# Feature projections of a linear attention on two row halves of TensorE, with a step order of its own

## The chip, the cores and the metric

The kernel runs on one core of a Trainium2 chip. A core has TensorE (matmuls, with weight loads that run beside them), VectorE, ScalarE, GpSimd, and SyncE, which here only issues DMA transfers. The profile calls them PE, PEld, DVE, ACT, POOL and SP. The metric is the device time of one execution in microseconds, the median of several executions.

## The reference, cut to what matters

Eight batches of eight heads, 576 tokens, head dimension 64, go through a linear attention with learned features; its output is the input of a mixture of eight experts, whose weights come from an iterated normalisation.

```
def phi(x):                                   # w_phi: 64 x 128
    proj = einsum('bhsd,df->bhsf', x, w_phi)
    proj = proj - max(abs(proj), axis=-1)
    return concatenate([exp(proj), exp(-proj)], axis=-1)
q_p, k_p = phi(q), phi(k)
kv = einsum('bhsf,bhsd->bhfd', k_p, v);  z = sum(k_p, axis=2)
attn = einsum('bhsf,bhfd->bhsd', q_p, kv) / (einsum('bhsf,bhf->bhs', q_p, z) + 1e-6)
x = attn as 4608 rows of 512
P = exp(x @ w_gate - max); 8 times: P /= P.sum(1); P /= P.sum(0); P *= N / E
out = sum over e of P[:, e] * (relu(x @ w1[e]) @ w2[e])
```

## The kernel before

**Attention.** The unit of work is a pair of heads of one batch: 32 pairs, four for each batch. Of a head's 576 tokens 512 are done with the pair, four chunks of 128; the last 64 tokens of all heads of a batch are done together as a remainder (`rest_a`). Two heads of 64 dimensions lie on the 128 partitions of a transposed tile `qkT` (`rT` for a remainder), the first head on partitions 0 to 63, the second on 64 to 127.

Each tile is projected in up to two ways. `tokens` (L583) puts tokens on the output partitions: each chunk of `qkT` is the stationary operand, and the weight moves. Keys need this for the features themselves, queries only for the largest absolute value of each token. `feature_rows` (L602) puts features on the output partitions, with the weight stationary and 512 tokens moving; queries need it. The weight is `wphi2`, [128, 2, 128], w_phi in one 64-row block and zeros in the other, so that one matmul over all 128 rows gives one head, or with both blocks moving, 256 columns, both heads of a chunk. The results fill two PSUM banks, from which VectorE takes maxima (L565) and ScalarE exponentials (L569). The constants in L403 choose among such layouts; `TI` is the one for two row halves, and it is 0 here.

GpSimd multiplies v by factors from the maxima (L761). `pair_b` forms kv (65 columns for a head: the values and the sum) and divides; the result is `xb`, tokens on partitions. `pair_c` (L877) turns `xb` into `xT`, the experts' input: in batches 2 to 6 by a transposing DMA issued on SP, otherwise by four transposes on TensorE and a copy out of PSUM on VectorE (L888).

**Inputs.** In batches 0 and 1, q and k come in fp32 over SP and are turned on TensorE. From batch 2 on, half a batch at a time, GpSimd issues the loads of q and k, which convert to bf16 (L501, two buffers), and SP issues the transposing DMA into `qkT` (L518, three buffers). SP also loads v. Queues run in the order in which instructions were issued to them; a DMA that waits holds all those behind it.

**Experts.** Expert 0 is plain: `up0` and `down0` make steps of 8 matmuls of 512 columns, on `xT` of one group of 512 tokens. 24 + 20 such steps are spread through attention; the others are done after it, beside the normalisation. From 258 us on experts 1 to 7 run with a seven-product scheme (L1273) to the end.

**What sets the order.** Two things. The string `order` (L1053) names steps: a, q and p are the key projection, the queries' maxima and the queries' features of a pair; b, n, m, c the rest of a pair; l, t, e, r, w loads, turns and remainders; g the gate; u and d expert 0. Each step records operations with an engine, an assumed duration, and the tiles and buffers they read and write. A list scheduler, `Plan.schedule` (L251), then simulates the engines and, again and again, starts the operation that can start first; ties go to the one recorded first. The sequence it finds is the program order of each engine. It knows of a mode of TensorE: `Clock.takes` (L178) charges 0.096 us where an operation marked `tiled` follows one that is not, or the reverse.

Of the kernel before, what the change touches and what calls it, by code (L numbers as in the profile page):

```python
# [10 lines left out]
BF16 = mybir.dt.bfloat16  # L11
# [180 lines left out]
class Plan:  # L192
# [58 lines left out]
    def schedule(self):  # L251
        ready = {}
        free = {}
        links, clock = Links(), Clock()
        for o in self.ops:
            if o.left == 0:
                ready.setdefault(o.eng, []).append(o)
        done = []

        def finish(o):  # L260
            for b in o.bufs:
                if b.ring.psum:
                    b.last = o
                b.left -= 1
                b.end = max(b.end, o.end)
                if b.left == 0:
                    b.ring.give(b.end, b.slot)
            for u in o.users:
                u.left -= 1
                u.ready = max(u.ready, o.after(u))  # L270
                if u.left == 0:
                    ready.setdefault(u.eng, []).append(u)

        while len(done) < len(self.ops) or links.next():
            best = None
            for eng, rq in ready.items():
                f = free.get(eng, 0.0)
                if best is not None and f > best[0]:
                    continue
                for o in rq:  # L280
                    t = self.start(o, f)
                    if t is not None and (best is None or (t, o.idx) < best[:2]):
                        best = (t, o.idx, o)
            landed = links.next()
            if landed and (best is None or landed[0] <= best[0]):
                o = links.land(*landed)
                o.end = landed[0] + 1.0
                finish(o)
                continue
            assert best is not None, "no operation can start"  # L290
            at, _, o = best
            ready[o.eng].remove(o)
            for b in o.bufs:
                if b.slot is None:
                    b.slot = b.ring.take(at)
            dur = clock.takes(at, o.dur, o.tiled) if o.eng == "PE" else o.dur
            free[o.eng] = at + dur
            if o.shared:
                self.port = at + dur
            done.append(o)  # L300
            if o.nbytes:
                links.add(o, at)
            else:
                o.stop = at + dur
                o.end = o.stop + o.lat
                finish(o)
        return done
# [9 lines left out]
def kernel(  # L317
# [11 lines left out]
    nc = tc.nc  # L329

    B, H, S, D = q.shape
    DF = w_phi.shape[1]
# [31 lines left out]
    a_in = tc.alloc_tile_pool(name="a_in", bufs=1)  # L364
# [3 lines left out]
    wphi_f = a_in.tile([128, DF], FP32, name="wphi_f")  # L368
    wphi2 = a_in.tile([128, 2, DF], BF16, name="wphi2")
    wphi2f = wphi2.rearrange("p a b -> p (a b)")  # L370

    vrd = [a_in.tile([128, 2, NP, 2, D1], BF16, name=f"vrd{i}") for i in range(2)]
    a_t = tc.alloc_tile_pool(name="a_t", bufs=1)
# [6 lines left out]
    def pe(cols, fn, r=(), w=(), takes=()):  # L380
        plan.op("PE", max(cols / 2400.0 + 0.0025, 0.031), 0.22, fn, r, w, takes)
# [4 lines left out]
    def dve(el, fn, r=(), w=(), shared=False):  # L386
        plan.op("DVE", el / 960.0 + 0.07, 0.15, fn, r, w, shared=shared)
# [7 lines left out]
    def dma(queue, nbytes, rate, fn, r=(), w=()):  # L395

        speed, unit = LINK.get(rate, (rate, 40))
        if nbytes == 2 << 20:
            speed, unit = 400, 150
        o = plan.op(queue, 0.8 if queue == "POOL" else 0.6, 0.0, fn, r, w, (), nbytes / speed)  # L400
        o.turn, o.unit = rate == 148, unit

    TI, GR, KM, QM, PM, NM, RM = 0, 0, 0, 0, 0, 0, 0  # L403
    R = {}

    wx = wp.tile([128, 8192], BF16, name="wx")
# [50 lines left out]
    def new(tag):  # L457
        return R[tag].new()

    def bf(buf):  # L460

        return buf().bitcast(BF16)
# [24 lines left out]
    def load_qk(b, hh, nh, t, r=()):  # L487

        o = hh % 4
        keys = [o // 2] if nh == 2 else [0, 1]  # L490
        if b < 2:
            g = t["f"]
            for x, src in ((1, k), (0, q)):
                i = 2 * x + o // 2
                dma("SP", nh << 17, 320, lambda x=x, src=src, i=i: nc.sync.dma_start(
                    out=acc[g][:, i:i + nh // 2].rearrange("p a (h c) -> p (a h) c", h=2),
                    in_=src[b, hh:hh + nh, 0:SM].rearrange("h (p j) d -> p h (j d)", j=NJ)),
                    r, [("acc", g, 2 * x + n) for n in keys])
            return
        for x, src in ((1, k), (0, q)):  # L500
            dma("POOL", nh << 17, 230, lambda x=x, src=src: nc.gpsimd.dma_start(  # L501
                out=t["qk"]()[:, x, o:o + nh],
                in_=src[b, hh:hh + nh, 0:SM].rearrange("h (p j) d -> p h (j d)", j=NJ)),
                r, [(t["qk"], x, i) for i in keys])
# [370 lines left out]
        return xb, outs  # L875

    def pair_c(b, pr, xb):  # L877
        if b in (2, 3, 4, 5, 6,):
            dma("SP", 1 << 17, 148, lambda: nc.sync.dma_start_transpose(
                out=xT[:, pr, b * SM:(b + 1) * SM].rearrange("p (a c) -> p a c", c=128),  # L880
                in_=xb()[:, 0:NJ].rearrange("p a b -> p (a b)")), [(xb, 0), (xb, 1)], [("xT", b, pr)])
            return
        pxt = new("P1")
        for j in range(NJ):
            pe(128, lambda j=j: nc.tensor.transpose(
                bf(pxt)[:, j * 128:j * 128 + 128], xb()[:, j, :], ident),
                [(xb, 0), (xb, 1), "ident"], [pxt])
        dve(270, lambda: nc.vector.tensor_copy(  # L888
            out=xT[:, pr, b * SM:(b + 1) * SM], in_=bf(pxt)[:, 0:512]),
            [pxt], [("xT", b, pr)])  # L890
# [103 lines left out]
    for i in range(2):  # L994
        dve(64, lambda i=i: nc.vector.tensor_copy(
            out=wphi2[64 * i:64 * i + 64, i, :], in_=wphi_f[64 * i:64 * i + 64, :]),
            [f"wphi_f{i}"], ["wphi2"])
    load_qk(0, 2, 2, halves[0, 0])
    load_rests(0, 1)
    load_v(0, 2, 2, halves[0, 0])  # L1000
# [2 lines left out]
    for i in range(2):  # L1003
# [4 lines left out]
        out=wgate_f, in_=moe_w_gate.rearrange("(c p) e -> p c e", p=128)), w=["wgate_f"])  # L1008
# [32 lines left out]
    def stage_g(b):  # L1041
# [4 lines left out]
    at = [0]  # L1046
# [4 lines left out]
             "c": lambda j: pair_c(j // 4, j % 4, xbs[j]), "g": stage_g,  # L1051
             "u": lambda i: up0(i // 4, i % 4), "d": lambda i: down0(i // 4, i % 4)}
    order = (  # L1053
        "lraeaepqbwlqaqawwabwmqlltnrbppnwqbppmrmanbqaqmwwacmpnpbccpwbtcnmqnaqbclupunm"
        "taumquglcapalbcpnqqdcenmucugbblnapmrcqdutabnqpmunpbambccddnqplanmqmducpblttb"
        "augnaqlnrbdcampcadmqeutunqcppmdcaqtdqabpbbmlrqtdnpmuaqualbnagnacctbmqulupran"
        "tdpmtdqcmdnpdabdancpcabbqmpumqbcdgnappqunburqcbugmmnqdcdanumupqbnucmcpnmbddp"
        "bqmpncncubncmmgccg"
    )
    for i, n in enumerate(order):  # L1060
        at[0] = i
# [22 lines left out]
    o = plan.op("X", 0.0, 0.0, swap, w=["late"])  # L1084
# [450 lines left out]
```

## Time and profile before

| | us |
|---|---|
| median of 8 runs | 1037.84 |
| lowest, highest | 1035.12, 1043.18 |
| the profiled execution | 1036.93 |
| its span, first to last instruction | 1035.1 |
| TensorE busy | 1014.6 |
| VectorE busy | 822.7 |
| ScalarE busy | 705.5 |
| GpSimd busy | 459.2 |

The span is what the engines show; the execution's own time has 1.8 us around it. Busy time is the time in which at least one instruction of an engine is in flight. Consecutive instructions overlap, so an engine that is shown as full may still have room, and what one instruction costs is read from the distance between the starts of neighbours rather than from its duration. Attention takes about the first fifth of the span: the last matmul that belongs to it ends near 212 us, and the rest of expert 0 fills the time to 258 us. A wait is put down to the engine or the DMA that ended it. The chain is the work that ended last, followed back from the last instruction.

### The profile page before, as it was taken

How to read it: one execution, taken by the hardware profiler on the slowest of the kernel's cores; microseconds unless marked ns; L12 is line 12 of the kernel's file. 1: busy time of each engine (PE TensorE's matmuls, PEld its weight loads, DVE VectorE, ACT ScalarE, POOL GpSimd, SP SyncE). 2: the span in 40 equal slices, each digit the busy share in tenths (PEclk: the TensorE clock that was granted, in tenths of full speed). 3: DMA queues.
4: the chain of work that ended last, by engine and by line, in shares of the span. 5: the costliest groups of instructions: out<-in, count | busy, mean ns of one | idle time of the engine just before them, and what ended most of it. 6: DMA issues, size and time to landing. Idle time of an engine off the chain costs nothing.

```text
span 1035.1 us, 24281 instructions
## 1 busy us (share of the span) xinstructions
PE 1014.6 (98%) x9488; PEld 838.6 (81%) x9488; DVE 822.7 (79%) x1596; ACT 705.5 (68%) x1530; POOL 459.2 (44%) x480
## 2 busy tenths in 40 slices
PE   7898999999999999999999999999999999999998
PEld 5665566654888888888888888888888888888885
DVE  7997798987788887778777877787778877787775
ACT  7998899943887866666666666666666566666663
POOL 5776665400243543344434443434444433444342
PEclk9999999999999999999999999999999999999999
DMA  9999989270222711161114311251116111614333
GB/s 251 191 183 182 152 135 143 57 154 1 92 83 84 153 41 42 42 126 39 48 45 95 81 42 42 53 120 34 53 42 133 43 42 42 124 41 125 131 123 123
DMA packets 114676, 96.56 MB, mean 93 GB/s; under 512 B 56320, under 2 KB 89216, under 8 KB 114560
## 3 DMA queue, kind: packets, MB, share of 16 engines
q1 hardware_dynamic: 82752, 71.08, 26.7%
q0 software_dynamic: 31648, 23.86, 16.5%
q8 instruction: 74, 1.21, 0.5%
q14 instruction: 42, 0.34, 0.1%
q10 hardware_dynamic: 160, 0.07, 0.0%
HBM read 94.98 MB, written 14.16 MB: 105 GB/s over the span
## 4 chain that ended last, share of the span: by engine, by line
PE 92%; DVE 2%; ACT 2%; DMA 2%; issue 1%; POOL 1%; SPq 0%; DVEq 0%; POOLq 0%; ACTq 0%
PE ps L1273 74%; PE ps L573 17%; PE ps L856 1%; DMA qkT<-qk 1%; DMA acc<-in_q_dram 1%; ACT k L569 1%; ACT q L569 1%; DVE m L565 0%; DVE ps L864 0%; DVE wx L565 0%; POOL v L761 0%; PE ps L703 0%; DVE xb L870 0%; ACT kr L569 0%; ACT wx L569 0%
## 5 line engine op out<-in xcount | busy, mean ns | idle before, releaser
L1428 POOL TENSOR_TENSOR acc<-acc,V 128x512 f32<-128x512 f32 x248 | 315.2, 1281 | 484.5 <-ACT V L1425 426.6
L1301 ACT COPY U<-ps 128x512 f32<-128x512 f32 x378 | 217.3, 587 | 166.2 <-PE ps L1273 151.0
L1305 DVE CUSTOM_DVE_ANT_0 hT<-ps,U 128x512 bf16<-128x512 f32 x378 | 254.4, 687 | 87.8 <-PE ps L1273 59.9
L1425 ACT ACTIVATE V<-ps,P 128x256 f32<-128x256 f32 x496 | 208.7, 474 | 90.1 <-PE ps L1273 82.2
L1413 DVE SCALAR_TENSOR_TENSOR acc<-ps,P,acc 128x256 f32<-128x256 f32 x372 | 159.0, 478 | 69.8 <-PE ps L1273 69.5
L1273 PEld LDWEIGHTS <-S 128*128 128x128 bf16 x1984 | 194.1, 98 | 22.9 <-issue 0.4
L1273 PEld LDWEIGHTS <-T 128*128 128x128 bf16 x1512 | 147.9, 98 | 17.2
L1273 PEld LDWEIGHTS <-hT 128*128 128x128 bf16 x1488 | 145.6, 98 | 16.9
L1273 PE MATMUL ps<-X,T 128*128 128x256 bf16 x1008 | 152.4, 273 | 0.0
L1273 PE MATMUL ps<-T,S 128*128 128x256 bf16 x1056 | 135.8, 273 | 0.1
L1273 PEld LDWEIGHTS <-wx 128*128 128x128 bf16 x1152 | 112.7, 98 | 13.6 <-issue 0.2
L1181 DVE TENSOR_TENSOR S<-hT 128x1024 bf16<-128x1024 bf16 x124 | 87.2, 712 | 10.1 <-ACT hT L1310 10.0
L1273 PEld LDWEIGHTS <-w 128*128 128x128 bf16 x864 | 84.5, 98 | 9.8
L1273 PE MATMUL ps<-xT,wx 128*128 128x256 bf16 x576 | 88.4, 273 | 0.1
L1273 PE MATMUL ps<-X,wx 128*128 128x256 bf16 x576 | 86.8, 273 | 0.0
L1310 ACT ACTIVATE hT<-ps 128x512 bf16<-128x512 f32 x126 | 73.3, 607 | 9.7 <-PE ps L1273 9.7
L573 PE MATMUL ps<-xT,w 128*128 128x512 bf16 x288 | 75.0, 383 | 3.0 <-DMA xT<-xb 3.0
L1273 PE MATMUL ps<-wx,hT 128*128 128x256 bf16 x560 | 77.6, 273 | 0.0
L1273 PE MATMUL ps<-xT,T 128*128 128x256 bf16 x504 | 76.7, 273 | 0.0
L573 PE MATMUL ps<-w,hT 128*128 128x512 bf16 x288 | 72.2, 381 | 0.0
L1273 PE MATMUL ps<-T,hT 128*128 128x256 bf16 x496 | 69.2, 273 | 0.0
L1273 PE MATMUL ps<-xT,w 128*128 128x256 bf16 x432 | 66.4, 273 | 0.0
(129 smaller groups left out, 1425.3 us busy)
## 6 DMA issues: line engine op xcount, KB each, us to landing
X<-xd SPq DMA_DIRECT2D x126, 256.0 KB, 2.7
wx<-in_moe_w_dram POOLq DMA_DIRECT2D x8, 1024.0 KB, 12.6
v_m<-in_v_dram SPq DMA_DIRECT2D x15, 512.0 KB, 6.0
out_dram<-acc SPq DMA_DIRECT2D x14, 512.0 KB, 3.1
w<-in_moe_w_dram POOLq DMA_DIRECT2D x6, 1024.0 KB, 11.7
xd<-S SPq DMA_DIRECT2D x18, 256.0 KB, 2.0
qk<-in_k_dram POOLq DMA_DIRECT2D x12, 256.0 KB, 5.2
qk<-in_q_dram POOLq DMA_DIRECT2D x12, 256.0 KB, 6.0
```

The lines of the kernel that those rows point to most:

```text
L569: act(el, lambda: nc.scalar.activation(out=dst(), in_=src(), func=ACT.Exp, bias=0.0, scale=scale), r, w)
L573: nc.tensor.matmul(out_, lhsT=lhsT, rhs=rhs, start=start, stop=stop)
L856: pe(65, lambda j=j: nc.tensor.matmul(pn()[:, j * D1:j * D1 + D1], lhsT=s["T"][x]()[:, j % 2, 2 * h + j // 2, :] if j < 4 else r["T"][x]() ...
L1181: lambda: f.tensor_tensor(out=out_(), in0=x(), in1=y(), op=op), r, w, **kw)
L1273: pe(256, lambda i=i, k=k, z=z: nc.tensor.matmul(bank()[:, 256 * i:256 * i + 256], lhsT=lhs(k, i), rhs=rhs(k), start=first and z, stop=k = ...
L1301: act(512, lambda: nc.scalar.copy(out=u[fp][n]().rearrange("p a b -> p (a b)"), in_=x[fp]()), [x[fp]], [u[fp][n]])
L1305: dve(515, lambda: nc.vector._custom_dve(ADD_SAT, out=out_(fp, i, j), in0=bank[fp]().rearrange("p (a b) -> p a b", a=2), in1=u[fp][n](), s ...
L1310: act(512, lambda: nc.scalar.activation(out=out_(fp, i, j), in_=x[fp]().rearrange("p (a b) -> p a b", a=2), func=ACT.Relu, bias=0.0, scale ...
L1413: dve(320, lambda n=n, ts=ts: nc.vector.scalar_tensor_tensor(out=acc[g][:, ts, 256 * j:256 * j + 256], in0=bank()[:, 256 * n:256 * n + 256 ...
L1425: act(370, lambda n=n: nc.scalar.activation(out=u()[:, n, :], in_=bank()[:, 256 * n:256 * n + 256], func=ACT.Copy, bias=0.0, scale=P[:, 4 ...
L1428: pool(695, lambda: nc.gpsimd.tensor_tensor(out=acc[g][:, 2 * i:2 * i + 2, 256 * j:256 * j + 256], in0=acc[g][:, 2 * i:2 * i + 2, 256 * j: ...
```

## The change

`TI` becomes 1, and a second weight tile `wphi` holds w_phi in both halves of the partitions, without zeros. A chunk is then projected by two matmuls of 64 rows and 128 columns, one for each half and so for each head, into two PSUM banks; the stationary feature projection becomes two matmuls of 64 rows and 512 columns. All matmuls of one such group are one operation for the scheduler, marked `tiled`. Each PSUM bank now holds one head with four chunks rather than two chunks of both heads, so the maxima and exponentials of a bank write every second block of their tiles. The remainders' 128-row feature projection (`wphi2[:, 0]`) stays as it was; their keys are done in two exponentials of 512 columns rather than four of 256.

In the scheduler, while TensorE's last operation was tiled, an untiled one counts as starting 0.096 us later when the next operation is chosen.

Batch 2 leaves the list of those whose output a DMA turns, so its four pairs are transposed on TensorE. The string `order` is another one; it has the same number of each step.

```
                     t = self.start(o, f)
-                    if t is not None and (best is None or (t, o.idx) < best[:2]):
-                        best = (t, o.idx, o)
+                    if t is None:
+                        continue
+                    key = t
+                    if eng == "PE" and o.tiled != clock.tiled:
+                        key += 0.096 if clock.tiled else 0.0
+                    if best is None or (key, o.idx) < best[:2]:
+                        best = (key, o.idx, o, t)
...
-            at, _, o = best
+            o, at = best[2:]
...
+    wphi = a_in.tile([128, DF], BF16, name="wphi")
...
-    TI, GR, KM, QM, PM, NM, RM = 0, 0, 0, 0, 0, 0, 0
+    TI, GR, KM, QM, PM, NM, RM = 1, 0, 0, 0, 0, 0, 0
...
     def pair_c(b, pr, xb):
-        if b in (2, 3, 4, 5, 6,):
+        if b in (3, 4, 5, 6,):
...
+    dve(64, lambda: nc.vector.tensor_copy(out=wphi, in_=wphi_f), ["wphi_f0", "wphi_f1"],
+        ["wphi"])
...
     order = (
-        "lraeaepqbwlqaqawwabwmqlltnrbppnwqbppmrmanbqaqmwwacmpnpbccpwbtcnmqnaqbclupunm"
-        "taumquglcapalbcpnqqdcenmucugbblnapmrcqdutabnqpmunpbambccddnqplanmqmducpblttb"
...
+        "leaawrqlrlwpaqatbwaqpeqqbpwanmmalwbawtppanmbbmcwpnqwmpalnlabaqmqncccuuqlncre"
+        "tpbmpbntqtcnapmlqqpbbapccqulbapbqrmbuqpualnnuunaqdmpanpnmqmltcbmtdrmubcbcden"
...
```

The layout that `TI` selects was in the file already:

```
    def tokens(pp, stat, n, r, takes=()):
...
        def rows():
            for c in range(n):
                for x in range(2):
                    nc.tensor.matmul(pp[1][x]()[:, 128 * c:128 * c + 128],
                                     lhsT=stat(c)[64 * x:64 * x + 64],
                                     rhs=wphi[64 * x:64 * x + 64], start=True, stop=True)

        o = plan.op("PE", n * 0.056, 0.22, rows, r + ["wphi"], pp[0], takes)
        o.tiled = 1
```

## The prediction

> **What bounds the kernel now.** I read the page's busy shares first, then busy time by stretches, then the waits and the chain of the first 212 us, since all that changes lies there. The stretches (columns: length, PE, PEld, DVE, ACT and POOL busy with instruction counts, granted clock, DMA share, GB/s):
>
> ```profile
> 0.00:60.00 60.00, 50.39 (x532) 34.53 (x533) 54.38 (x117) 54.59 (x135) 42.53 (x74) 1.00 1.15 223
> 60.00:90.00 30.00, 30.00 (x365) 19.98 (x364) 28.00 (x67) 29.18 (x73) 22.53 (x37) 1.00 1.30 169
> 90.00:112.00 22.00, 16.53 (x176) 10.38 (x173) 13.26 (x32) 13.82 (x34) 10.49 (x17) 0.84 1.22 177
> 112.00:212.00 100.00, 99.60 (x1144) 64.40 (x1142) 89.15 (x207) 92.83 (x223) 56.95 (x93) 1.00 0.68 112
> 212.00:258.00 46.00, 46.00 (x251) 21.30 (x248) 37.62 (x99) 17.04 (x30) 1.73 (x2) 1.00 0.41 87
> ```
>
> From 212 us on TensorE never rests, and nothing after that is changed: 207 matmuls of expert 0 stand behind the last gate before, 205 in the changed program's order. So the time moves by as much as the end of attention, now at 212 us, moves. Before it there are four regimes. To 60 us ScalarE and VectorE are full and TensorE waits 9.6 us: a lighter TensorE buys nothing. In 60:90 and 112:212 TensorE is full and ScalarE has 0.8 + 7.2 = 8.0 us to spare. In 90:112 nobody is full: that is a stall.
>
> The waits of the first 212 us (engine, line, releaser: us in total, times, longest) and the chain through the stall (start, us, what):
>
> ```profile
> POOL qk L501 <- PE ps L573: 6.4, 4, 5.5
> POOL qk L501 <- DMA qkT<-qk: 3.5, 1, 3.5
> PE ps L573 <- DMA xT<-xb: 3.0, 1, 3.0
> PE ps L573 <- POOL v L767: 2.6, 2, 2.5
> ```
>
> ```profile
> 92.42 0.66 DVE xb L870 x2
> 93.72 1.82 DMA xT<-xb
> 95.53 7.57 DMA qkT<-qk
> 103.66 0.80 POOL qk L501
> 104.49 1.57 POOL v L761
> ```
>
> TensorE stood 3.0 us before an expert 0 matmul that reads xT of batch 2, which a DMA turned (issue to landing 4.1 to 7.1 us here). On SP the turn of q and k (95.53) stood behind such a transpose, and the next load of q and k and then the v product stood behind that turn on POOL. In 90:112 TensorE idled 22.00 - 16.53 = 5.5 us, and its granted clock was 0.84, another 22 x 0.16 = 3.5 us: 9.0 us in all.
>
> Durations of the projections and of what is nearest to them:
>
> ```profile
> 152.49 0.60 PE L573 MATMUL ps<-wphi,qkT 128*128 128x256 bf16 x4
> 150.24 0.59 PE L573 MATMUL ps<-qkT,wphi 128*128 128x512 bf16 x2
> 203.24 0.39 PE L885 MATMUL ps<-ident,xb 128*128 128x128 bf16 x4
> L573 PE MATMUL ps<-wgate,xT 128*128 128x8 bf16 x144 | 4.9, 166 | 0.0
> ```
>
> Matmuls overlap, so what one costs is the distance between starts. The next matmul after each row's group starts 0.44, 0.43 and 0.22 us after it: 109 ns for one of 256 columns, 215 for 512, 55 for 128.
>
> **The change part by part.**
>
> *Projections on row halves.* In the kernel before, 288 matmuls of 256 columns and 64 of 512 (with the 8 of rT, which stay whole, 72) go through a weight that is half zeros. The changed program has 576 of 128 columns and 64 of 512, each on 64 rows, neighbours on opposite halves. If a pair runs at once it takes what one takes: 55 ns for 109, 215 for 431. No row of before shows two halves together. The ends: full overlap, a gain of 54.5 ns a token matmul and 215 a feature pair; none, 576 x 55.5 = 32.0 against 31.4 us, a loss of 0.6. I take full overlap, because the two halves share neither rows, weights nor PSUM bank. Where TensorE is full, in 60:90 (first three rows) and 112:212, there are
>
> ```profile
> L573 PE MATMUL ps<-wphi,qkT 128*128 128x256 bf16 x41 | 6.7, 272 | 0.0
> L573 PE MATMUL ps<-qkT,wphi 128*128 128x512 bf16 x12 | 4.0, 378 | 0.0
> L573 PE MATMUL ps<-wphi,rT 128*128 128x256 bf16 x4 | 0.6, 273 | 0.0
> L573 PE MATMUL ps<-wphi,qkT 128*128 128x256 bf16 x120 | 18.4, 272 | 0.2 <-DVE m L565 0.2
> L573 PE MATMUL ps<-qkT,wphi 128*128 128x512 bf16 x32 | 9.4, 379 | 0.0
> L573 PE MATMUL ps<-wphi,rT 128*128 128x256 bf16 x12 | 1.8, 273 | 0.0
> ```
>
> 41 + 4 + 120 + 12 = 177 token matmuls and 12 + 32 = 44 feature matmuls, that is 22 pairs: 177 x 0.0545 + 22 x 0.2155 = 9.6 + 4.7 = 14.4 us. The rest lies before 60 us, hidden behind ScalarE and VectorE, or in the stall; without that cover it would be a further gain.
>
> *Switching between whole array and halves.* In the built order of the changed kernel the tiled matmuls stand in 74 runs, so TensorE switches 148 times; a share of 177/288 of them, 91, lies where it is full. No row prices a switch. The ends: nothing, or the whole depth of the pipe, as the 128x8 row shows it: 166 ns long against 25 between starts, 0.141 us. It cannot gain. I take the middle, 0.07, as no row stands nearer to either end: 6.4 us (0 to 12.8). The 0.096 in the scheduler is its own assumption and is not used.
> The Trainium skill, TensorEngine Tiling (Array Packing), Key Properties, speaks against the change here: a change of tiling mode "drains the TensorE". No run here has shown one. By that rule the switches cost 12.8 us and the sum below is -3.5 in place of -9.9.
>
> *Batch 2 on TensorE again.* Adds 16 transposes of 55 ns, 0.9 us where TensorE is full, and four copies on VectorE of 0.415 us (1.7 us, hidden: VectorE idles 8.7 us in 90:112; 1.7 lost if that cover goes). SP loses four transposes that held it 1.25 + 1.71 + 1.94 + 1.21 = 6.1 us, and the turns, loads and rT transposes behind them come sooner. The wait of 3.0 us on xT of batch 2 goes: a transpose and a copy replace a landing of 4 to 7 us. What is late next is the turn of 7.57 us, so I take -3.0, with 0 and -9.0 (the whole stall) as ends.
>
> *New order, and the scheduler's preference.* Only the places of instructions. On POOL the twelve loads of q and k stand, counted in pairs by which they precede their first user, 4 5 4 5 5 6 6 7 7 5 5 5 before and 6 5 3 4 4 6 5 7 7 7 8 8 after: the third to fifth are closer. Taken at zero, with a stall as the upper end (a rival below) and the rest of the old stall as the lower.
>
> *Small edits with one answer.* One more copy of the weight on VectorE ahead of the first projection: 0.22 us by the row of its sister L995 (4.02 and 5.69 us), all on the path at the start: +0.2. The eight remainder batches need 16 exponentials of 512 columns for 32 of 256, 0.48 against 0.26 us apart: ScalarE is spared 0.8 us, counted as nothing. Strided writes of the halves have the same run of 128 elements: nothing.
>
> **Sum.** -14.4 + 6.4 + 0.9 - 3.0 + 0.2 = -9.9 us. The profiled execution took 1036.93 us (span 1035.1); it becomes 1027.0. It stood 0.9 below the median of 1037.84, so I say 1027.9. Of the -7.1 that TensorE gives, ScalarE's 8.0 us to spare lets all through, but no more than that.
> The same page, PSUM Bottleneck, warns that the reading out of PSUM may become the limit once TensorE is sped up. The row agrees as far as ScalarE's 92.83 of 100 goes; the estimate by the rule would keep of the sum only the -3.0 + 0.2.
>
> **The rivals.**
>
> *B, the stall goes entirely.* For it: both named waits begin at batch 2's transposes. Against: the stretch shows DMA at 1.22 of its share, and turn and loads remain. With ScalarE's room used up: -8.0 - 9.0 = -17.0, 1020.8.
>
> *C, TensorE's gain turns into idle time.* ScalarE and VectorE are 93% and 89% busy in 112:212 and may hold the order. For it: 0:60 looks like that already. Against: TensorE had 0.4 us of idle there. -3.0 + 0.2, and any one new wait of that size: 1035 to 1038, say 1036.
>
> *D, the halves do not overlap.* Tokens +0.3 where TensorE is full, features nothing, switches +6.4, transposes +0.9, with -3.0 + 0.2: +4.8, 1042.6. It decides from a token pair of 92 ns on in place of 55 (a feature pair of 0.36 us), where 4.5 of the 14.4 us are left. For it only that no row shows the overlap.
>
> *E, a new stall earlier.* The third load now precedes its user by 3 pairs of 6.2 us (32 pairs from 9.8 to 203.2 us), 18.7 us. In before that load took 15.7 us from issue (56.54) to the turn's landing (72.26), the fifth 19.1, the sixth 22.3. If two of the third to fifth are late by enough to stall as now, 2 x 9.0 - 9.9 = +8.1, 1045.9. It decides from 13 us of new stall on. Against: six turns now precede the first transposed output on SP, where it was four.
>
> **How the numbers follow.** Forecast 0.38, B 0.16, C 0.13, D 0.13, E 0.20. What a measurement of this kernel can tell from no change is about 0.3%, 3.1 us. Faster is the forecast and B, 0.54; same C, 0.13; slower D and E, 0.33. The forecast's own range is 1024 (ScalarE's 8.0 and 5.9 of the stall) to 1034 (full drains). For 8 in 10 it reaches from 1017, somewhat below B, to 1046, which takes in D and E's mean.
>
> **What would show it.** Tiled matmuls of 128 columns that start in pairs, 55 ns from pair to pair, show the first step right; 110 show D. The gap at a switch beyond the usual distance is its price; over 0.18 us each, 91 of them eat the whole gain. No wait of TensorE on a DMA into xT around 90 us shows the third step; a clock below 1.00 anywhere in the first 200 us shows a stall that is left or new. ScalarE at 97% or more with TensorE under 95% between 112 us and the end of attention would show C. The forecast is wrong if attention does not end between 198 and 209 us.

## The result, and the profile after

The changed kernel takes 1040.77 us (median of 17 runs, 1038.18 to 1044.92), the kernel before 1037.12 us (median of 46). The ratio is 1.0036, with a 95% interval of 1.0025 to 1.0047: slower by 0.36%, just beyond what a measurement can tell. Forecast was 1027.9. The profiled execution of the changed kernel took 1040.77 us, its span 1039.0 us, and the clock granted to TensorE was 0.992 over the span, 0.996 before.

Busy time by stretches of the changed kernel (columns: length, PE, PEld, DVE, ACT and POOL busy with instruction counts, granted clock, DMA share, GB/s):

```profile
0.00:60.00 60.00, 48.84 (x662) 33.64 (x662) 54.84 (x124) 54.15 (x128) 40.48 (x72) 0.97 1.06 217
60.00:90.00 30.00, 27.84 (x342) 15.13 (x337) 25.55 (x59) 25.50 (x61) 22.00 (x34) 1.00 1.10 163
90.00:112.00 22.00, 19.18 (x239) 11.33 (x238) 18.14 (x40) 19.67 (x47) 12.59 (x21) 0.92 1.19 168
112.00:212.00 100.00, 93.70 (x1224) 55.43 (x1224) 84.16 (x195) 87.27 (x212) 57.09 (x94) 0.95 0.77 114
212.00:258.00 46.00, 46.00 (x290) 22.20 (x287) 37.99 (x103) 18.70 (x34) 1.72 (x2) 1.00 0.40 86
```

The two regimes in which TensorE was full have gone. It idles 30.00 - 27.84 = 2.2 us in 60:90 and 6.3 us in 112:212, where it idled 0.0 and 0.4; the stall of 90:112 shrank from 5.5 to 2.8 us, and before 60 us it idles 11.2 for 9.6. The granted clock, which was below 1.00 only in 90:112, is below it in three stretches. The other engines did not take over: in 112:212 ScalarE fell from 92.83 to 87.27 us and VectorE from 89.15 to 84.16.

For every kernel below I account for attention in the same three terms. Its end is the start of its last matmul. Idle time is time with no matmul of TensorE in flight. Clock lost is each stretch's length times what its granted clock lacks to 1.00. The rest is TensorE's work.

| | attention ends | work | idle | clock lost |
|---|---|---|---|---|
| before | 211.8 | 192.9 | 15.5 | 3.4 |
| after | 216.5 | 185.6 | 22.4 | 8.5 |

The change took 7.3 us of work out, and 6.9 us of idle time and 5.1 of clock came in: +4.7 us. The terms are good to about a microsecond. Idle time while the clock is at half counts in two columns, which makes the work 0.5 us too small in the changed kernel and 1.2 in e1 below. And at the start, until 9.2 us before and 7.9 after, matmuls stand at twice their usual distance (213 ns for 109) without a listed clock: 2.6 and 1.9 us that lie in the work. Experts 1 to 7 start at 262.5 us, where it was 258.2, and from there the two traces run alike.

Some of the waits of the changed kernel's first 220 us (engine, line, releaser: us in total, times, longest):

```profile
POOL qk L507 <- DMA qkT<-qk: 11.2, 3, 5.5
PE ps L601 <- ACT wx L575: 3.3, 1, 3.3
PE ps L579 <- POOL v L773: 2.8, 2, 2.3
POOL qk L507 <- PE ps L891: 2.5, 1, 2.5
```

The 3.0 us that TensorE waited for a DMA into `xT` is gone. In its place the loads of q and k on GpSimd wait 11.2 us for the turn of an earlier half batch, where it was 3.5. The chain through attention (start, us, what) now goes through those turns:

```profile
71.78 12.03 DMA qkT<-qk x2
...
95.36 10.75 DMA qkT<-qk
106.67 0.80 POOL qk L507
107.50 1.79 POOL v L767
...
119.30 13.28 DMA qkT<-qk
...
134.08 7.71 DMA qkT<-qk
```

A turn (`DMA qkT<-qk`) must land before the load that takes its source buffer can be issued, and on GpSimd's queue the product of v stands behind that load. The turn that was issued at 119.30 took 13.3 us; four remainder loads issued beside it, at 119.53 to 121.61, took 10.3 to 11.2 us each. In the whole chain the turns' share rose from 0.7% to 4.2%. SP's instructions at that place, and then GpSimd's two loads that waited (start, us, engine, line, operation; in brackets the wait before it and its releaser):

```profile
119.30 5.78 SPq L524 DMA_TRANSPOSE qkT<-qk  x1
126.69 2.16 SPq L885 DMA_TRANSPOSE xT<-xb  x1
132.57 1.34 SPq L643 DMA_TRANSPOSE rT<-qk_r  x1
134.08 4.73 SPq L524 DMA_TRANSPOSE qkT<-qk  x1
```

```profile
133.13 0.85 POOL L507 DMA_DIRECT2D qk<-in_k_dram  x1 [2.80 <-DMA qkT<-qk]
142.35 0.81 POOL L507 DMA_DIRECT2D qk<-in_k_dram  x1 [5.48 <-DMA qkT<-qk]
```

Two neighbouring turns were issued 14.8 us apart, and both held up a load.

The halves themselves, in TensorE's own list (start, us, engine, line, operation):

```profile
160.81 0.59 PE L579 MATMUL ps<-xT,w 128*128 128x512 bf16 x2
161.34 0.40 PE L601 MATMUL ps<-wphi,qkT 64*128 64x128 bf16 x8
161.66 0.29 PE L579 MATMUL ps<-vrd,kr 128*128 128x130 bf16 x2
...
162.40 0.39 PE L619 MATMUL ps<-qkT,wphi 64*128 64x512 bf16 x2
162.63 0.39 PE L601 MATMUL ps<-wphi,qkT 64*128 64x128 bf16 x8
```

Eight matmuls of 128 columns take 0.32 us until the next operation starts, and two of 512 columns 0.23. Within a group the two halves of a pair start 3 to 6 ns apart, and the first and the eighth start of a token group lie 181 ns apart: three steps from pair to pair, 57 to 60 ns each. The halves overlap fully.

### The profile page after: what moved, and what is told of

It reads as the page before. It is cut to its first block, busy times and chain, and to the rows that moved or that the text cites. A ratio compares the mean times of both kernels' runs of the same rounds, so it can differ in the third digit from the quotient of the medians.

```text
span 1039.0 us, 24854 instructions
## 1 busy us (share of the span) xinstructions
PE 1012.0 (97%) x9792; PEld 827.6 (80%) x9792; DVE 823.7 (79%) x1601; ACT 703.1 (68%) x1514; POOL 458.8 (44%) x480
## 4 chain that ended last, share of the span: by engine, by line
PE 87%; DMA 4%; ACT 3%; DVE 2%; POOL 2%; issue 1%; POOLq 0%; DVEq 0%; ACTq 0%
PE ps L1281 73%; PE ps L579 11%; DMA qkT<-qk 4%; PE ps L862 1%; PE ps L601 1%; ACT wx L575 1%; DVE m L571 1%; ACT q L575 1%; ACT k L575 1%; POOL v L767 1%; POOL qk L507 1%; PE ps L619 0%; DVE ps L870 0%; POOL vrd L689 0%; DMA acc<-in_k_dram 0%
## 5 line engine op out<-in xcount | busy, mean ns | idle before, releaser
L1433 ACT ACTIVATE V<-ps,P 128x256 f32<-128x256 f32 x496 | 208.3, 473 | 90.8 <-PE ps L1281 82.8
L579 PE MATMUL ps<-w,hT 128*128 128x512 bf16 x288 | 76.8, 387 | 0.1
## 6 DMA issues: line engine op xcount, KB each, us to landing
wx<-in_moe_w_dram POOLq DMA_DIRECT2D x8, 1024.0 KB, 12.2
```

The costliest lines, as they stand in the source:

```text
L579: nc.tensor.matmul(out_, lhsT=lhsT, rhs=rhs, start=start, stop=stop)
L1433: act(370, lambda n=n: nc.scalar.activation(out=u()[:, n, :], in_=bank()[:, 256 * n:256 * n + 256], func=ACT.Copy, bias=0.0, scale=P[:, 4 ...
```

## The experiments

The first theory was that the halves gain what was worked out and the new order loses more (1). Against it stood that the halves are worth nothing where they stand (2), and that the old kernel's schedule happened to be a good one that any edit spoils (3). The reading above added that late turns of the inputs eat the gain. All medians are in us; "before there" is the kernel before on the same chip in the same set of runs.

| run | median (n) | before there | ratio, 95% interval | end, idle, clock lost |
|---|---|---|---|---|
| e1 whole array, same places | 1044.83 (6) | 1036.94 | 1.0070 (1.0055 to 1.0084) | 220.4, 20.8, 6.8 |
| e2 old order, batch 2 by DMA | 1040.98 (10) | 1036.94 | 1.0028 (1.0010 to 1.0047) | 218.2, 28.5, 5.1 |
| e3 old order | 1041.08 (9) | 1036.94 | 1.0036 (1.0024 to 1.0049) | 215.8, 24.1, 6.8 |
| e4 third buffer | 1035.99 (12) | 1036.94 | 0.9978 (0.9959 to 0.9997) | 208.1, 19.0, 3.4 |
| e5 third buffer in before | 1034.22 (12) | 1036.70 | 0.9972 (0.9959 to 0.9986) | 208.3, 14.8, 1.7 |
| e6 no preference | 1052.66 (4) | 1036.70 | 1.0148 (1.0124 to 1.0172) | 232.1, 27.5, 11.9 |
| e7 batch 2 by DMA | 1041.20 (12) | 1036.70 | 1.0042 (1.0020 to 1.0063) | 220.0, 24.1, 5.1 |
| e8 third buffer, scheduled | 1041.85 (10) | 1036.70 | 1.0045 (1.0027 to 1.0063) | 220.5, 23.0, 5.1 |
| e9 batch 2 only | 1026.99 (4) | 1036.65 | 0.9907 (0.9894 to 0.9920) | 202.5, 11.7, 0.0 |
| e10 one price | 1034.85 (12) | 1036.65 | 0.9987 (0.9973 to 1.0001) | 208.8, 16.2, 1.7 |
| e11 third buffers of qk and v | 1037.48 (12) | 1036.65 | 1.0003 (0.9982 to 1.0023) | 208.1, 21.4, 3.4 |
| e12 the same in before | 1037.61 (12) | 1036.65 | 0.9999 (0.9985 to 1.0013) | 212.9, 19.3, 3.4 |
| e17 e9 with copies | 1026.61 (6) | 1036.21 | 0.9907 (0.9890 to 0.9924) | 202.8, 10.0, 0.0 |
| e18 e3 with copies | 1035.48 (12) | 1036.21 | 0.9993 (0.9980 to 1.0006) | 212.4, 20.7, 5.1 |
| e19 groups, whole array | 1037.43 (12) | 1036.21 | 1.0009 (0.9994 to 1.0025) | 211.3, 16.8, 0.0 |
| e20 e19's places, halves | 1038.76 (12) | 1036.21 | 1.0023 (1.0011 to 1.0035) | 213.5, 20.1, 5.1 |
| e21 e17, one price | 1030.08 (5) | 1037.29 | 0.9937 (0.9924 to 0.9951) | 205.1, 11.4, 0.0 |
| e22 after, with copies | 1025.10 (4) | 1037.29 | 0.9888 (0.9875 to 0.9902) | 200.3, 12.6, 1.7 |

The last column comes from one profiled execution each, the median from all. The profiled executions of e4 (1032.25 us) and e11 (1032.45) lie well below their medians; e4's twelve runs fall into four from 1030.1 to 1032.3 and eight from 1035.1 to 1037.9, and its profile shows one of the four. In e6, e7 and e8 the time from attention's end to expert 1 is 42.6 to 42.9 us, where it is 46.0 to 46.8 in the others, so their ends read 3 to 4 us too late beside them.

### e1: the changed kernel, the same instructions in the same places, on the whole array

```
-                                     lhsT=stat(c)[64 * x:64 * x + 64],
-                                     rhs=wphi[64 * x:64 * x + 64], start=True, stop=True)
+                    nc.tensor.matmul(..., lhsT=stat(c),
+                                     rhs=wphi2[:, x, :], start=True, stop=True)
...
-                nc.tensor.matmul(..., lhsT=wphi[half], rhs=mov()[half],
+                nc.tensor.matmul(..., lhsT=wphi2[:, x, :], rhs=mov(),
```

> The changed kernel with every instruction of every engine in the same place, but each projection matmul over the whole array again: 8 of 128 columns against the zero-padded weight for a key or maxima group, 2 of 512 for the features, no switches. TensorE's work rises by 288 x 0.055 + 32 x 0.2155 = 22.7 us less 148 x 0.095 = 14.1 us of switches, 8.6 us in all. Theory 1 (the halves pay, and the new order's late turns of q and k lose it again): 3 to 9 us slower than the changed kernel, 1044 to 1050. Theory 2 (attention is held by ScalarE and the inputs whatever TensorE does, so halves are worth nothing): within 2 us of the changed kernel, 1039 to 1043.

Without the halves 1044.83 us, with them 1040.77: they gain 4.1 us by the medians, 3.5 by the ratios. TensorE's work is 192.8 us without and 185.6 with: 7.2 us less, of which attention's end keeps 220.4 - 216.5 = 3.9. Theory 2 in its plain form falls. But the whole array in these places is 7.9 us slower than the kernel before, so the places themselves cost more than the halves give.

### e2, e3, e7: the old order, with and without batch 2 on TensorE

```
-        "leaawrqlrlwpaqatbwaqpeqqbpwanmmalwbawtppanmbbmcwpnqwmpalnlabaqmqncccuuqlncre"
+        "lraeaepqbwlqaqawwabwmqlltnrbppnwqbppmrmanbqaqmwwacmpnpbccpwbtcnmqnaqbclupunm"
...
```

e3 is the changed kernel with the old `order` alone. e2 has that and the old line of `pair_c`; e7 has that line alone, with the new order:

```
-        if b in (3, 4, 5, 6,):
+        if b in (2, 3, 4, 5, 6,):
```

> The kernel before with its own step order and batch 2 turned by DMA, plus the row halves and the scheduler's preference. Theory 1 (the loss is the new order's): the old order's single stall stays, TensorE has some 5 to 8 us less to do, 1029 to 1034. Theory 2 (halves are worth nothing): 1035 to 1040. A third outcome, slower than 1041, would say that the halves themselves bring the stalls, since they reshuffle what the scheduler does with the same steps.

> The whole change except for the step order: row halves, preference, batch 2 turned on TensorE, old order. Theory 1: 1026 to 1034, as forecast, with no wait of TensorE on a DMA into xT of batch 2. Theory 2: 1035 to 1040.

> The changed kernel with batch 2's output turned by DMA as before, the new step order kept. If batch 2 on TensorE relieves SyncE's queue as forecast: a wait of TensorE on a DMA into xT comes back and the run is 2 to 6 us slower than the changed kernel, 1043 to 1047. If its return to TensorE gains nothing: 1039 to 1043.

1040.98, 1041.08 and 1041.20 us: in the old order the halves are as slow as in the new one, with or without batch 2. Theory 1, the new order alone at fault, falls: the changed kernel and e3 differ in the order alone and stand 0.3 us apart. In the old order, too, idle time is high with the halves (24.1 us in e3) and 6.8 us of clock are lost. Batch 2's return to TensorE is worth nothing beside the halves, 0.4 us by e7 and -0.1 by e2 against e3.

### e6: without the scheduler's preference

```
                     key = t
-                    if eng == "PE" and o.tiled != clock.tiled:
-                        key += 0.096 if clock.tiled else 0.0
```

> The changed kernel without the scheduler's preference for the current mode: 180 switches in place of 148. At the 0.095 us that the trace shows for a switch, 32 x 0.095 = 3.0 us more work on TensorE. If that alone counts: 1 to 3 us slower than the changed kernel, 1042 to 1044. As all engines' orders shift with it, stalls may differ: a difference over 5 us either way would be put down to those, read from the waits on turns of q and k.

1052.66 us, 12 more than the changed kernel. TensorE then switches 180 times for 148, which at 0.095 us each (measured below) is 3.0 us. The rest is no switch: idle time is 27.5 us for 22.4, the clock lost 11.9 for 8.5. The preference moves many operations, and most of its gain lies there. How each of them moved was not followed.

### e4, e5, e8, e11, e12: more buffers for the loads

In e4, at unchanged places, the loads of q and k go round over three buffers instead of two. The third is a view of a tile that is free then.

```
+    loads, own_qk = [0], R["qk"].make
+    def third(slot):
+        loads[0] += 1
+        if loads[0] % 3:
+            return own_qk(loads[0] % 3 - 1)
+        return acc[4][:, 0:2, :].rearrange("p a b -> p (a b)").bitcast(BF16).rearrange(
+            "p (x h c) -> p x h c", x=2, h=4)
+    R["qk"].make = third
```

> The changed kernel in its own instruction order, but the loads of q and k rotate through three buffers (the third lies in an accumulator that is unused until late), so a load on GpSimd's queue waits for the turn three loads back instead of two. Theory 1 (the stalls at 80 to 92 and 130 to 150 us come from loads that hold GpSimd's queue until a late turn has freed the buffer, 11.2 us in three waits): those waits go, 4 to 10 us faster, 1031 to 1037. If the turns themselves are late because of DMA and SyncE's queue alone: within 2 us, 1039 to 1043.

1035.99 us, 4.8 less by the medians and about 6 by the ratios, with attention's end at 208.1 for 216.5 in the execution that was profiled. The waits of GpSimd's loads on turns are gone, and one wait of TensorE itself on a turn shows in their place. In e4's waits of the first 220 us:

```profile
PEld L611 <- DMA qkT<-qk: 5.7, 1, 5.7
PE ps L611 <- DMA qkT<-qk: 5.2, 1, 5.2
```

The weight load and the matmul of one token projection (L611 here) waited for it, until 90.0 us. So the buffers carried part of the loss, and the turn's own lateness carries another.

e5 is the same edit on the kernel before; in e8 the scheduler knows of the third buffer and moves the loads with it (`R["qk"].free.append((0.0, 2))`); e11 and e12 are e4 and e5 with a third buffer for v as well.

> The kernel before, every instruction in its place, with the same third buffer for q and k that took 4.8 us off the changed kernel. If holding up GpSimd's queue is what the changed kernel has and before hardly has (two named waits, 9.9 us, one stall): a gain of 0 to 4 us, 1033 to 1037, so most of the 4.8 belongs to the new schedule. If the buffer is a limit of both alike: 4 to 8 us faster, 1029 to 1033, and the halves then bring nothing beside it.

> The changed kernel with the third buffer known to the scheduler too, so that loads of q and k are also issued earlier. If late inputs are what is left of the stalls: faster than the third buffer alone, 1029 to 1035. If the earlier loads only collide with the turns on the DMA engines: 1035 to 1042.

> The changed kernel in its own instruction order with a third buffer for q and k and a third for v, so that a load of v holds SyncE's queue, and the turns behind it, less. 11.9 us of SyncE's time went to v loads that waited for GpSimd. If turns are late behind those: 2 to 6 us less than with the third q and k buffer alone (1036.0), 1030 to 1034. If turns are late by the DMA engines alone: 1035 to 1037.

> The kernel before in its own order with both third buffers. The stall that is left with the third q and k buffer is TensorE's wait of 4.2 us on a DMA into xT of batch 2, which v loads hold up little: 1031 to 1035. It tells whether the changed kernel, freed of its queue waits in the same way, comes out ahead: by theory 1 the changed one is 2 to 5 us faster here.

The kernel before gains 2.5 us in e5, less than the changed kernel; TensorE's wait on batch 2's output stays there (4.2 us, once). Scheduled, the third buffer gives nothing (1041.85), and a third buffer for v gives nothing either; neither is a direction that helps by itself. With e5 at 1034.22 and e4 at 1035.99 the change is still not faster once both have the buffer.

### e9, e10: batch 2 alone, and one price

```
-        if b in (2, 3, 4, 5, 6,):
+        if b in (3, 4, 5, 6,):
```

> The kernel before with batch 2's output transposed on TensorE and nothing else: whole array, old step order. By the step as forecast: the wait of TensorE on a DMA into xT (3.0 us) goes, +0.9 us of transposes, 1034 to 1036. If the place of every instruction, which the scheduler shifts with any edit, matters more than the edit: anywhere from 1037 to 1047, with other stalls than before.

1026.99 us, ratio 0.9907: this one line of the change, in the kernel before, is worth 9.7 us and makes the fastest kernel of those that leave nothing out. Its busy time by stretches (the columns as above):

```profile
60.00:90.00 30.00, 29.68 (x367) 20.42 (x371) 28.38 (x70) 29.02 (x73) 23.40 (x38) 1.00 1.25 175
90.00:112.00 22.00, 21.79 (x260) 14.55 (x261) 20.61 (x49) 20.59 (x52) 14.70 (x26) 1.00 1.10 187
112.00:202.00 90.00, 89.15 (x1038) 58.59 (x1052) 81.64 (x190) 85.10 (x207) 52.86 (x85) 1.00 0.72 117
```

The stall of 90:112 is gone, 0.2 us of idle time for 5.5 and the clock at 1.00 for 0.84. Nothing has come in its place. The DMA share of that stretch is still 1.10 (1.22 before) at 187 GB/s (177 before), so it was not the volume of transfers. What the edit takes away are batch 2's transposing DMAs, on which TensorE waited and behind which the turns stood on SP; which of the two counts for more was not tried.

In e10 the scheduler's price of every ScalarE operation goes up by a nanosecond, which changes nothing but places:

```
-        plan.op("ACT", max(el / 1200.0 + 0.058, 0.107), 0.22, fn, r, w)
+        plan.op("ACT", max(el / 1200.0 + 0.059, 0.107), 0.22, fn, r, w)
```

> The kernel before with one assumed price in the scheduler changed by 1 ns (58 to 59 ns of fixed cost of a ScalarE instruction). No instruction is added or taken away; only places shift. Theory 3 (the step order of before was chosen for the exact schedule that it gives, and any other schedule of the same steps has some microseconds more of stalls): 2 to 10 us slower than before, 1039 to 1047. If schedules of the same steps are alike: 1036 to 1038.

1034.85 us, ratio 0.9987, not told apart from 1. This chance shift of the old schedule did not cost 4 us; theory 3 falls in the form that any edit spoils it.

### e17, e18, e21, e22: every turning DMA replaced by a plain copy

All turning DMAs, those of q and k, of the remainders and of the output, become plain ones of the same size from the same to the same tiles, so that nothing is transposed by DMA and the values are not the reference's. TensorE, VectorE and ScalarE do what they did.

```
-            dma("SP", 1 << 19, 148, lambda: nc.sync.dma_start_transpose(
-                out=t["T"]().rearrange("p a b c -> p (a b) c"),
+            dma("SP", 1 << 19, 148, lambda: nc.sync.dma_start(
+                out=t["T"]().rearrange("p a b c -> p (a b c)"),
...
```

e22 does this to the changed kernel, e17 to e9, e18 to e3, and e21 to e9 with e10's price.

> The changed kernel (1040.8), every instruction in its place, with plain copies in place of its turning DMAs; the copy does not transpose, so other numbers are computed. If the loss in its own order is inputs turned late: the half-clock stretches at 93, 138 and 144 us go, 6 to 12 us faster, 1029 to 1035. If it lies between the engines: 1037 to 1041.

> Batch 2 on TensorE, old step order, whole array (1027.0 us with turning DMAs), with every turning DMA replaced by a plain copy of the same bytes between the same tiles, in the same place and with the same waits; the copy does not transpose, so the numbers that are computed are others. It is the yardstick of the next three. Its stalls were gone already: 1022 to 1028.

> Row halves, batch 2 on TensorE, old step order (1041.1 us with turning DMAs), with the same copies in place of turning DMAs. If the 14 us that halves lose against batch 2 alone are inputs turned late: they go, and the halves' lighter TensorE shows, 1016 to 1026, faster than the yardstick. If they lie between the engines (groups that take two banks, prices, order): it stays 4 to 14 us slower than the yardstick, 1027 to 1040.

> Batch 2 on TensorE, old step order, whole array, copies in place of turning DMAs as in the yardstick (1026.6), and the scheduler's assumed fixed cost of a ScalarE instruction 59 ns for 58, so that the places of instructions shift. If schedules of the same operations are alike: within 3 us, 1024 to 1030, and the grouping's 10.8 us are its own. If the yardstick is one lucky schedule: 1032 to 1040.

e22 takes 1025.10 us: with quick turns the changed kernel is 15.7 us faster (15.3 by the ratios). Its stretches:

```profile
60.00:90.00 30.00, 28.98 (x356) 15.76 (x354) 28.50 (x64) 29.10 (x69) 25.99 (x43) 1.00 1.08 194
90.00:112.00 22.00, 21.99 (x301) 12.72 (x298) 20.30 (x48) 22.00 (x54) 14.92 (x23) 1.00 0.90 186
112.00:212.00 100.00, 99.91 (x1296) 59.12 (x1294) 91.78 (x222) 87.71 (x210) 52.98 (x88) 1.00 0.53 120
```

TensorE is full again, or within 1.0 us of it, where it was full before, with the halves in place. From issue to landing (bytes where the form gives them, median us), the twelve transfers went from the first of these rows, of the changed kernel, to the second, of e22:

```profile
qkT<-qk SPq DMA_TRANSPOSE x12, 6.2
```

```profile
qkT<-qk SPq DMA_DIRECT2D x12, 512.0 KB, 4.8
```

Summed over the twelve, 89.4 us became 55.7. The loads beside the turns landed sooner too: the medians of k and q went from 5.9 and 7.4 us to 4.8 and 6.1. So e22 shows what transposing by DMA costs in these places, in the turns and in what runs beside them; the two are not separated. In e9 the same replacement changes nothing (1026.61, though the sum fell from 71.4 to 57.0 us), so there no turn is late. The theory of late turns holds for the new order: that is where its gain went. In the old order with the halves it holds in part: e18 gains 5.6 us over e3 (4.5 by the ratios), and stays 8.9 above e17, with no wait on a turn longer than 1.1 us left. With copies the new order is 10.4 us faster than the old one (e22 against e18); with the turns the two stand 0.3 us apart. e21 shows a chance shift at this place: 3.5 us over e17, so with copies 7.2 us (1037.29 - 1030.08) of batch 2's gain stay at other places.

### e19, e20: the grouping without the halves

Switching `TI` on does more than use halves: a group is one operation, it holds two PSUM banks at once, and a bank holds one head. e19 is e17 with these groups, but on the whole array and priced so. e20 is e19, in the same places, on the halves, with 166 switches. Both have copies for the turns.

```
-    TI, GR, KM, QM, PM, NM, RM = 0, 0, 0, 0, 0, 0, 0
+    TI, GR, KM, QM, PM, NM, RM = 1, 0, 0, 0, 0, 0, 0
...
+                    nc.tensor.matmul(pp[1][x]()[:, 128 * c:128 * c + 128], lhsT=stat(c),
+                                     rhs=wphi2[:, x, :], start=True, stop=True)
+        plan.op("PE", n * 0.11, 0.22, rows, r + ["wphi"], pp[0], takes)
...
+        plan.op("PE", 0.432, 0.22, rows, r + ["wphi"], pt[0])
```

> Copies in place of turning DMAs, batch 2 on TensorE, old step order, whole-array matmuls at whole-array prices, but one operation for each projection that takes both PSUM banks at once, and a bank for each head. If grouping costs by itself: 4 to 14 us over the yardstick. If it is harmless: within 3 us of it.

> The same with every instruction in the same place, the projections on row halves, 166 switches. TensorE has 22.7 - 166 x 0.095 = 6.9 us less to do than in the run with the whole array in these places. If halves gain in any order: 2 to 6 us faster than it.

e19 takes 1037.43 us against e17's 1026.61: in this order the grouped kernel is 10.8 us slower, three times the one chance shift of e21, with no half and no switch in it. Part of it lies early. In 20:80 and 80:217, first e17, then e19:

```profile
20.00:80.00 60.00, 56.45 (x709) 39.49 (x709) 58.33 (x137) 59.03 (x149) 45.10 (x75) 1.00 1.01 197
80.00:217.00 137.00, 137.00 (x1540) 87.44 (x1537) 123.91 (x297) 121.95 (x293) 78.95 (x127) 1.00 0.64 137
```

```profile
20.00:80.00 60.00, 52.24 (x726) 37.21 (x724) 51.33 (x122) 52.58 (x123) 42.31 (x69) 1.00 0.86 173
80.00:217.00 137.00, 134.90 (x1732) 89.68 (x1731) 125.29 (x292) 123.44 (x295) 82.46 (x133) 1.00 0.62 132
```

In 20:80 of e17 ScalarE was 59.03 us busy, full; in e19 it is 52.58, and no other engine is full in its place. e20 is 1.3 us above e19, and their intervals overlap: in those places the halves gain nothing. What in the grouping costs this (two banks taken at once, one head to a bank, or the places into which the scheduler shifts everything) is not separated by these runs and stays open. It was measured in the old order only: e22 is grouped as well and stands 1.5 us below e17, so in the new order no such cost shows. That grouping is also what keeps e3 behind e9 fits the 8.9 us that e18 leaves, but is argued, not shown: e18 schedules other places.

## Why the prediction was wrong, step by step

**That the time moves with attention's end** was right: the end moved by +4.7 us, the profiled execution by 1040.77 - 1036.93 = +3.8. By the prediction's own sign, an end between 198 and 209 us, the forecast failed: it was 216.5.

**The halves** were right as work, not as time. Full overlap was taken, and pairs start 57 to 60 ns apart, 3 to 6 ns within a pair. The work in attention fell by 7.3 us in the traces and 7.2 in e1 against the whole array. The four pairs of a token group and the feature pair cost what was worked out. Rival D falls with it. In time the halves gave 3.5 to 4.1 us in the new order (e1) and nothing in e20's places.

**The switches** were undersized. From the distances between starts (the rows from 160.81 us above have one: 0.53 us for two matmuls of 512 columns is 0.215 + 0.311), a 512-column matmul before a tiled one took 311 ns to the next start instead of 215, a tiled token group before a whole matmul 148 instead of 55, a 65-column one before a tiled one 125 instead of 29: 0.093 to 0.096 us a switch, each way. I took 0.07, the middle of 0 and 0.141; over 91 switches that is 8.6 us for 6.4, an error of 2.3 us. Over all 148 it is 14.1 of the 22.6 us that the halves save. A token group that stands alone, 4 pairs and 2 switches, costs 0.42 us against 0.436 on the whole array, so it gains nothing; only groups that stand together do. The Trainium skill, TensorEngine Tiling (Array Packing), Key Properties, says without a figure that a change of mode drains the array; these rows agree, and give about two thirds of the whole depth that I had as the upper end.

**Batch 2** was undersized too, in the other direction. I took -3.0 us, with the whole stall, -9.0, as the end; alone it measured -9.7 (e9), beyond that end. The wait that I thought late next, the turn of 7.57 us, did not stay late: it had itself stood behind batch 2's transposes on SP. That is rival B's mechanism, and it is the part that was left out of the likeliest case for want of following the queue one link further. The -9.7 holds for the kernel before alone: beside the halves the same line gave 0.4 us or less (e7, and e2 against e3).

**New order and preference, "taken at zero"**, is the step that failed, as a statement on the places of instructions: that the change moves them and that this costs nothing. One edit after the other, the runs give -9.7 us for batch 2 (e9), +14.1 for all that comes with `TI` in the old order (e3 against e9), where halves and switches stood at -14.4 + 6.4 = -8.0 in the sum, and -0.3 for the new order (the changed kernel against e3). So the exchange of one order for the other did come out at zero, but by luck: with copies it is worth -10.4 us (e22 against e18), and the late turns take that back.

Three things lay in the places. First, in the new order the turns are late: the transposing DMAs cost 15.7 us there by e22. That is rival E's mechanism. The count of pairs between load and user was a sign of it only in part. The chain shows late turns at the third and fourth (71.78 and 76.32 us), two of the three that E named, but worse ones at the sixth, eighth and ninth (95.36, 119.30 and 134.08), where the count is the same as before (6, 7 and 7); the seventh, which the count has closer too (5 for 6), is not among them. E's price of 1045.9 overshot. The reason I gave against it, that six turns precede the first transposed output instead of four, counted only the order on SP and not which load waits for the turn to land. Second, the operations that the halves come in are larger and take their banks together. That had no term in my sum. In the old order the kernel with it is 10.8 us slower on the whole array (e19 against e17); in the new order no run shows it. Third, and in the other direction, the preference is worth 12 us (e6), of which the switches are 3.

With quick turns the changed kernel stood 1037.29 - 1025.10 = 12.2 us below the one before. My sum was -9.9, and that the two are near is luck. Batch 2 alone reaches 1026.99 without halves, and 1026.61 with copies: it makes up 9.7 of the 12.2, where the sum had 0.9 - 3.0 = -2.1 for it. All the rest of the change is worth 1.5 us with quick turns (e22 against e17; 2.0 by the ratios, whose intervals overlap), where the sum had -8.0 for halves and switches. Why so little of their 7.3 us of work shows even then stays open. The kernel before was not run with copies.

**ScalarE's room and rival C.** ScalarE did not become the bound, nor did VectorE: both are emptier in 112:212 than before. C's form, idle time that eats the gain, came (+6.9 us), but its cause, engines that are too full, did not. The Trainium skill, TensorEngine Tiling (Array Packing), PSUM Bottleneck, warns of that cause; no run here shows it in 112:212, e22 least, where TensorE is 99.91 of 100 us busy with ScalarE at 87.71.

**The small edits** were not measured alone.

**The clock** was counted in the old stall (3.5 of its 9.0 us) and else named as a sign, not as a cost. 8.5 us were lost to it, 5.1 more than before, beside 6.9 us of idle time that came in, and no term of the sum allowed for it.

What stays: batch 2 on TensorE in the kernel before, 1026.99 us, beats both kernels.

## What to carry to other kernels

Before a new step order is put at zero, follow each load from its issue to the buffer it waits for and to what is queued behind it; here a lighter TensorE in front of late transfers gave back as idle time (6.9 us) what it gained (7.3). Cost a mode switch for each group, not for each matmul: here two switches cost nearly as much as a group of four pairs saves. And when a change comes as a bundle, run its smallest line alone: here one line was worth 9.7 us alone, and next to nothing inside the bundle.

## What the runs showed of the hardware

**The clock falls without a long pause.** I had taken a clock below 1.00 as the mark of a stall. Three consecutive windows of 3.4 us of the changed kernel (columns as above):

```profile
11.30:14.70 3.40, 1.67 (x16) 1.10 (x17) 2.85 (x5) 3.40 (x11) 2.33 (x5) 1.00 1.07 339
14.70:18.10 3.40, 3.40 (x28) 2.41 (x27) 2.54 (x4) 3.40 (x11) 3.35 (x6) 0.50 1.11 288
18.10:21.50 3.40, 2.89 (x40) 1.89 (x37) 3.26 (x6) 3.40 (x10) 2.90 (x10) 1.00 1.28 239
```

In the first, TensorE has an operation in flight for 1.67 of 3.40 us, and the array works 35% of it, counted as matmuls times the usual distance between their starts; its longest pause is 1.03 us. The next window has half the clock. The same follows 32% in e22, from 12.9 us, with a pause of 1.36 us at the window's end; 35, 33 and 36% in e18, with longest pauses of 0.95, 0.87 and 1.23 us; and 35% in e20 (0.88 us), where it lasted 10.2 us. Windows of 42% and more at full clock kept it, with one exception, and between 38 and 41% it went either way. The exception is in the kernel before: the window from 104.8 us, 44% by this count, opened with a pause of 1.8 us, and half the clock followed at 108.2. The window ahead of that kernel's loss at 98 us was nearly empty, 7%. So the share of work is a sign, and not shown to be the whole rule. It suggests that a lighter TensorE pays twice, since the halves do the same work in less of the window. e1, with the whole array in the same places, lost no clock before 60 us after the start-up, nor did the other eight kernels without halves; of the eleven with halves nine did, and e4 and e8 did not. These are single profiles. The Trainium skill, TensorE: Matmul & The Clock Gate, has two statements on this. Its Part 1 gives an idle window of about 3.4 us as what lowers the clock again; the window's length agrees with these rows, that it must be idle does not. Its section on a second failure mode says that many small pauses between groups of matmuls can do it too; the rows agree that pauses shorter than the window suffice, and add the share of work, about 36% or less.

**A switch of mode has one price.** 0.093 to 0.096 us in either direction, after matmuls of 65, 128 or 512 columns, and 0.090 to 0.104 from a feature pair back to the whole array.

**A turn by DMA has no fixed time.** Of the same 512 KB, one took 4.2 and another 13.3 us from issue to landing, the latter beside four loads. Plain copies in their place had a median of 4.5 to 4.8, from 2.9 to 7.2.
